# Layer 1's first products of two token tiles by seven block products in place of eight, and all element-wise work behind attention on VectorE

## The chip, the cores and the metric

The kernel runs on one core of a Trainium2 chip. The metric is the device time of one execution, in microseconds (us). Times named "profiled" are those of one execution that the hardware profiler recorded. Engines: TensorE (PE, with its weight loads as PEld), VectorE (DVE), ScalarE (ACT), GpSimd (POOL), and SyncE (SP), which here only issues transfers.

## The reference

Linear attention with decay over blocks of 64 tokens, then two feed-forward layers on the 1536 tokens x 512 channels that it gives. The two layers are where most of the work lies:

```python
x = attn_out.transpose(0, 2, 1, 3).reshape(1536, 512)
h = x @ w_in                                    # 512 x 2048, layer 0
g = np.where(h > 0.0, h, np.exp(np.minimum(h, 0.0)) - 1.0)
x = g @ w_out                                   # 2048 x 512
h = x @ w_in2                                   # layer 1
g = np.maximum(h, 0.0) + np.log1p(np.exp(-np.abs(h)))
out = g @ w_out2
```

## The kernel before

**Tiles and chunks.** Tokens lie in three tiles of 512 (t = 0, 1, 2), the 2048 inner channels of a layer in 16 chunks of 128 (c). For each layer, tile and chunk there is a first product (`hps`, 128 x 512, over 512 input channels in four parts), an activation, and a second product that is added to the tile's four accumulators `y`. A value of 32 bits is split into a high and a low part (`xh`, `xl`; `wih`, `wil`; `woh`, `wol`; `g`), and each product is three matmuls (`product`, lines 387 to 389; `m2_part`, line 437). A first product is thus 12 matmuls, a second product too.

**Stages.** Attention runs first, with the first eight chunks of tile 0 between its steps (`early_step`). Behind it `build` makes a list of operations `Op` for all the rest, and `schedule` puts them in order: it plays the operations with a table of assumed durations, keeps a list of ready ones for each engine, and writes each engine's instructions in the order in which they began. TensorE chooses between two sequences, first products (`m1_seq`) and second ones (`m2_seq`). On the chip each engine then runs its own list in order and waits where an operand or a buffer isn't ready. `PLAN` is the order of the chunks: four chunks of tile 0 (`one`), then two pairs of chunks for tiles 1 and 2 (`two` or `fast`).

**A fast pair.** `quick` computes the first products of two chunks for tiles 1 and 2, which are a 2 x 2 block product (halves of the input channels by the two chunks), with seven products of half the depth, six matmuls each, instead of four of 12. It works on sums of weight halves (`sum_ops`, tiles `sumsw`, split into `s0h`, `s0l`, `s1h`, `s1l`) and on sums of token halves (`t1` to `t4`, high and low parts). Products go to the banks `pa`, `pb` and `pd`; copies and adds of VectorE and ScalarE (`copy_op`, `add_op`, tiles `p1`, `u2`, `p5`) combine them. In each pair the sixth product (`t3`) ends on `pa`, an add on VectorE reads `pa`, and only then may the seventh (`t4`) go on in that bank. In the kernel before, layer 0 has seven fast pairs, layer 1 none. Layer 0's token sums are made from the halves of x behind attention (`first_sums`).

**Activation.** Layer 0: two steps on ScalarE, one on VectorE (line 450). Layer 1: |h| (`e`, line 741), exp, + 1 (`u`) and log (line 754) on ScalarE; then u − 1 − e (line 758), v − u (line 545), max(h, 0) + v (line 764). Then ScalarE copies the high part of `g` and the low part is v − g (line 545). Nine buffers `v` hold values in work, three hold `g`.

**VectorE or GpSimd.** The operations through `minus` and `plus` (lines 545 and 548), such as the low parts, v − u and the sums, could go to either engine in the kernel before: the one that was free first in the scheduler's play took it.

**The end.** The last accumulators are evicted (line 1099) and stored by SyncE; a `probe` of 15 matmuls stands behind the last second product.

Of the kernel before, what the change touches and what calls it, by code (L numbers as in the profile page):

```python
# [9 lines left out]
F32 = mybir.dt.float32  # L10
# [22 lines left out]

FAST = (True, False)

# [20 lines left out]
def body(ctx, tc, lamc, attqk, attkv, w1, w2, out):  # L56
# [398 lines left out]
    order = count()  # L455

    class Op:

        def __init__(self, on, key, fn, after=(), gate=None, end=None):
            self.on, self.key, self.fn, self.gate, self.done = on, key, fn, gate, end  # L460
            self.then, self.wait, self.n, self.gone, self.first = [], 0, next(order), False, False
            self.behind(*after)
            ops.append(self)
# [7 lines left out]
    def schedule(pe, free):  # L471
# [3 lines left out]
        heads = [0] * len(pe)  # L475
        pool = [0.0]

# [6 lines left out]
        def begin(op, e):  # L484
            op.gone = True
            took = op.on[e]
            if e == "V" and isinstance(took, tuple):
                took, both = took
                if both and pool[0] > now:
                    over = pool[0] - now  # L490
                    took = over + took - SHARE * over if SHARE * over < took else took / SHARE
            if e == "G":
                pool[0] = now + took
            op.fn(e) if len(op.on) > 1 else op.fn()
            busy, late = took if isinstance(took, tuple) else (took, took)
# [8 lines left out]
        while left:  # L504
            now, _, op = heappop(events)
            if op is not None:
                left -= 1
                if op.done:
                    op.done()
                for nxt in op.then:  # L510
                    nxt.wait -= 1
                    if nxt.wait == 0:
                        enter(nxt)
            if events and events[0][0] <= now:
                continue
            if free["P"] <= now:
                m2_seq, m1_seq = pe
                ahead = list(takewhile(lambda o: o.wait == 0, m2_seq[heads[0]:heads[0] + 8]))
                can = [bool(ahead), heads[1] < len(m1_seq) and m1_seq[heads[1]].wait == 0]
                can[1] = can[1] and (m1_seq[heads[1]].gate is None or m1_seq[heads[1]].gate())  # L520
                if can[0] and (not can[1] or sum(o.on["P"] > MM3 for o in ahead) + sum(o.on["P"] == MM3 for o in ahead) // 4 >= PILE and not m1_seq[heads[1]].first):
                    pick = 0
                else:
                    pick = 1 if can[1] else None
                if pick is not None:
                    heads[pick] += 1
                    begin(pe[pick][heads[pick] - 1], "P")
            for e in "SAGV":
                if free[e] > now:
                    continue  # L530
                ready[e] = [x for x in ready[e] if not x[2].gone]
                for x in ready[e]:
# [17 lines left out]
    engines = {"V": V, "G": G}  # L550
    both = {"G": TT_G, "V": TT_V}
    half = {"G": 0.76, "V": (0.42, True)}
    wide = {"G": 2.7, "V": (1.28, True)}

    def build():
# [54 lines left out]
        def weights_ops():  # L610
            for k, task in enumerate(tasks):
# [45 lines left out]
                o2 = Op({"A": SCALAR}, key, a2, [o1, summed_[t1] if t1 else None])  # L657
                o3 = Op({"V": 0.55}, key, v1, [o1])
                o4 = Op({"V": 0.75}, key, v2, [o3, o2])
                o5 = Op({"A": SCALAR}, key, a3, [o4])  # L660
                o6 = Op(W_LO, key, v3, [o5])
                loads[task] = ld, o2
# [51 lines left out]
        def act_ops(key, src, after, done):  # L714

# [3 lines left out]
            if layer == 0:  # L719
# [12 lines left out]
                o = Op({"A": SCALAR}, k, x2, [o])  # L732
                o = Op({"V": PS_V}, k, x3, [o], end=done)
            else:
# [33 lines left out]
                o = Op({"A": SCALAR}, k, s2, [o])  # L768
                o = Op(PLUS_ONE, k, s3, [o])
                o4 = Op({"A": SCALAR}, k, s4, [o])  # L770
                o5 = Op({"V": PS_V}, k, s5, [o4])
                o6 = Op(SOFT, k, s6, [o5], end=lambda: eu.append(box["i"]))
                o = Op({"V": PS_V}, k, s7, [o6], end=done)

# [9 lines left out]
            h = Op({"A": SCALAR}, k, hi, [o, m2_last.get(queue[j - 3])])  # L784
            low = Op(V_LO, k, lo, [h], end=lambda: vfree.add(box["k"]))
            for p in m2_ops[key]:
# [43 lines left out]
        def sum_ops(q):  # L830
# [26 lines left out]

            o0 = Op(W_SUM, k0, g0, deps)
            o1 = Op(W_HALF, k0, g1, deps)
            o2 = Op(W_HALF, k0, g2, deps)  # L860
            o3 = Op(W_HALF, k0, lambda e: plus(e, cut(0), cut(3), cut(0)), [o1, o2])
            o4 = Op(W_HALF, k1, lambda e: minus(e, cut(3), cut(1), cut(3)), [o0, o3])
            o5 = Op(W_HALF, k0, lambda e: minus(e, cut(1), cut(0), cut(1)), [o4])
            o6 = Op(W_HALF, k1, lambda e: minus(e, cut(2), cut(2), cut(1)), [o5])
            out_ = []
            for i, key, deps in ((0, k0, [o5, o3]), (1, k1, [o6, o4])):
# [16 lines left out]
        def quick(layer, p):  # L883
# [47 lines left out]
            def copy_op(src, tag, key, after):  # L931
# [33 lines left out]
            held["s", 0], held["s", 1] = [p5, p6], [p3, p7]  # L965
            held["p1"] = [act_ops(keys[0, 1], lambda: box["p1"], [a11], None)]
            held["u2"] = [act_ops(keys[0, 2], lambda: box["u2"], [a12], None)]
            held["p5"] = [act_ops(keys[1, 2], lambda: box["p5"], [a22], None)]
            act_ops(keys[1, 1], lambda: box["a"], [p4], lambda: give_bank(box["a"]))
# [12 lines left out]
        def part_ops(i, k, f, key, deps, new):  # L982
# [10 lines left out]
            h = Op({"A": SCALAR}, key, hi, deps)  # L993
            return h, Op(T_LO, key, lo, [h])

        def first_sums(plain_end):
# [10 lines left out]
            def chain(name, key, deps, *terms):  # L1007
                o = None
                for i, (fn, a, b) in enumerate(terms):
# [67 lines left out]
        def unit_ops(u):  # L1077
# [8 lines left out]
            for m in range(KD):  # L1086
# [15 lines left out]
                if fresh:  # L1102
# [21 lines left out]
        def split_ops(t):  # L1124
# [4 lines left out]
            for m in range(KD):  # L1129
# [10 lines left out]
                prev = h if m == 0 else prev  # L1140
                xdone[1, t].append(Op(V_LO, key0 + m * MM3 - 3.0, lo, [h]))
            held["acc", t] = list(xdone[1, t])


# [12 lines left out]
        def close_units(keys_done):  # L1157
            while made_units[0] < len(units) and all(k in keys_done or queue.index(k) < EARLY for k in units[made_units[0]]):
# [4 lines left out]
                if t in ysplit and (1, t) not in xdone:  # L1163
                    split_ops(t)

# [45 lines left out]
    def close_attention():  # L1211
# [3 lines left out]
        late["tp"] = ctx.enter_context(tc.tile_pool(name="ltp", bufs=1, reuse_waits="tile"))  # L1215

    def probe():
        ps = pp.tile([P, TT], F32, tag="b0", name="probe")
        a, x = halves["i", 2 * NF - 1][0][:, 0:P], xh[0][0]
        b = x.rearrange("p a n -> p (a n)")  # L1220
        for n in (256, 384, 512):
            for i in range(5):
                T.matmul(ps[:, :n], a, b[:, :n], start=True, stop=True, skip_group_check=True)

# [125 lines left out]
```

## Time and profile before

| | us |
|---|---|
| median of three runs | 591.49 (590.26 to 592.46) |
| the profiled execution's own time | 590.46 |
| its span from the first to the last instruction | 588.7 |
| TensorE busy | 573.4 |
| VectorE busy | 414.9 |
| ScalarE busy | 368.4 |
| GpSimd busy | 316.7 |

The span is 1.8 us shorter than the execution's own time, and that time 1.0 us shorter than the median. A matmul's record overlaps the next one's, so that a busy TensorE shows only where it did not wait.

### The profile page before, as it was taken

To read this page: it belongs to the slowest core of one execution; us is meant where nothing else is said; L and a number is where in the kernel's file an instruction comes from. 1 tells how busy PE (TensorE), PEld (TensorE's weight loads), DVE (VectorE), ACT (ScalarE), POOL (GpSimd) and SP (SyncE) were. 2 spreads that over 40 slices of the span, in tenths; PEclk is the share of its full clock that TensorE was granted. 3 is DMA by queue.
4 is the path that set the end of the run, shared out by engine and by line. 5 is a ranking of instruction groups with operands and counts; after the bars stand their busy time and mean duration, and the time that the engine had idled before them with its cause. 6 is when DMAs were issued, how large, how long until landed. Compare 5 with 4: busy or idle time off the path is not lost.

```text
span 588.7 us, 8054 instructions
## 1 busy us (share of the span) xinstructions
PE 573.4 (97%) x2999; PEld 467.9 (79%) x2999; DVE 414.9 (70%) x546; ACT 368.4 (63%) x652; POOL 316.7 (54%) x246
## 2 busy tenths in 40 slices
PE   8899999979999989999999999999999999999999
PEld 7777778757788878888888788887888887888887
DVE  6678778999868398845887937687785479633732
ACT  1365657647876667645868568887794488464720
POOL 4634356998755374544374835547453555343541
PEclk9999999989999999999999999999999999999999
DMA  8944642101214122420223102132223011000023
GB/s 317 409 165 126 243 157 90 37 0 36 73 45 135 38 70 72 144 72 1 84 96 107 37 1 72 36 108 71 73 71 108 1 37 36 1 0 1 0 85 130
DMA packets 14582, 49.80 MB, mean 85 GB/s; under 512 B 1744, under 2 KB 1744, under 8 KB 14544
## 3 DMA queue, kind: packets, MB, share of 16 engines
q1 hardware_dynamic: 14544, 49.30, 24.3%
q8 instruction: 23, 0.38, 0.3%
q14 instruction: 15, 0.12, 0.1%
HBM read 46.14 MB, written 3.15 MB: 84 GB/s over the span
## 4 chain that ended last, share of the span: by engine, by line
PE 63%; DVE 20%; ACT 5%; DMA 5%; POOL 3%; issue 3%; SPq 0%; DVEq 0%; ACTq 0%
PE y L437 31%; PE hps L387 8%; PE hps L388 8%; PE hps L389 8%; DMA raw<-w 4%; DVE r L164 2%; PE pa L387 2%; PE pa L389 2%; PE pa L388 2%; DVE sums L545 2%; DVE u L758 2%; DVE v L450 2%; DVE r L642 2%; DVE r L637 2%; DVE yacc L1099 1%
## 5 line engine op out<-in xcount | busy, mean ns | idle before, releaser
L545 POOL TENSOR_TENSOR g<-v,g 128x512 fp32r<-128x512 f32 x69 | 96.1, 1393 | 98.2 <-ACT g L777 98.2
L437 PE MATMUL y<-g,woh 128*128 128x512 f32 x384 | 119.4, 392 | 0.8 <-ACT yacc L1094 0.8
L437 PE MATMUL y<-woh,g 128*128 128x512 f32 x384 | 118.2, 389 | 0.0
L777 ACT ACTIVATE g<-v 128x512 fp32r<-128x512 f32 x89 | 56.1, 631 | 73.7 <-PE y L437 68.6
L545 POOL TENSOR_TENSOR v<-v,u 128x512 f32<-128x512 f32 x38 | 52.9, 1392 | 61.7 <-DVE u L758 61.7
L437 PEld LDWEIGHTS y<-g,woh 128*128 128x128 f32 x384 | 71.6, 188 | 17.1 <-ACT yacc L1094 1.6
L437 PEld LDWEIGHTS y<-woh,g 128*128 128x128 f32 x384 | 72.1, 188 | 14.9
L387 PE MATMUL hps<-xh,wih 128*128 128x512 f32 x200 | 79.6, 398 | 0.8 <-DVE v L764 0.6
L388 PE MATMUL hps<-xl,wih 128*128 128x512 f32 x200 | 78.3, 391 | 0.4 <-POOL xl L545 0.4
L389 PE MATMUL hps<-xh,wil 128*128 128x512 f32 x200 | 78.1, 391 | 0.0
L437 PE MATMUL y<-g,wol 128*128 128x512 f32 x192 | 74.8, 389 | 0.0
L437 PE MATMUL y<-wol,g 128*128 128x512 f32 x192 | 74.7, 389 | 0.0
L1099 DVE TENSOR_TENSOR yacc<-y,yacc 128x512 f32<-128x512 f32 x68 | 45.4, 687 | 35.9 <-PE y L437 35.8
L758 DVE SCALAR_TENSOR_TENSOR u<-u,e 128x512 f32<-128x512 f32 x48 | 43.6, 908 | 32.4 <-ACT v L754 32.4
L642 DVE CUSTOM_DVE_ANT_0 r<-r,c 128x1024 uint16<-128x1024 uint16 x49 | 46.8, 956 | 6.7 <-ACT c L632 6.1
L387 PEld LDWEIGHTS hps<-xh,wih 128*128 128x128 f32 x200 | 37.8, 189 | 11.8 <-DVE v L764 2.7
L764 DVE SCALAR_TENSOR_TENSOR v<-hps,v 128x512 f32<-128x512 f32 x48 | 32.8, 684 | 18.2 <-POOL v L545 18.0
L388 PEld LDWEIGHTS hps<-xl,wih 128*128 128x128 f32 x200 | 37.8, 189 | 8.2 <-POOL xl L545 0.8
L389 PEld LDWEIGHTS hps<-xh,wil 128*128 128x128 f32 x200 | 37.7, 188 | 7.9
L437 PEld LDWEIGHTS y<-wol,g 128*128 128x128 f32 x192 | 36.0, 188 | 7.5
L437 PEld LDWEIGHTS y<-g,wol 128*128 128x128 f32 x192 | 36.0, 188 | 7.5
L741 ACT ACTIVATE e<-hps 128x512 f32<-128x512 f32 x48 | 28.2, 587 | 16.0 <-PE hps L389 15.0
(198 smaller groups left out, 1158.4 us busy)
## 6 DMA issues: line engine op xcount, KB each, us to landing
raw<-w SPq DMA_DIRECT2D x64, 512.0 KB, 3.7
qk<-attqk SPq DMA_DIRECT2D x8, 512.0 KB, 7.0
kv<-attkv SPq DMA_DIRECT2D x8, 512.0 KB, 7.0
out<-yacc SPq DMA_DIRECT2D x12, 256.0 KB, 2.1
early<-attkv SPq DMA_DIRECT2D x2, 512.0 KB, 9.2
early<-attqk SPq DMA_DIRECT2D x2, 512.0 KB, 10.6
earlykv<-attkv SPq DMA_DIRECT2D x2, 512.0 KB, 10.9
earlyqk<-attqk SPq DMA_DIRECT2D x2, 512.0 KB, 10.9
```

What stands on the lines that cost most here:

```text
L164: V.tensor_tensor(out=ri, in0=ri, in1=c, op=ALU.add)
L387: T.matmul(ps, wh[:, wo[i]], xa[i], start=(start and i == 0), stop=False, skip_group_check=True)
L388: T.matmul(ps, wh[:, wo[i]], xb[i], start=False, stop=False, skip_group_check=True)
L389: T.matmul(ps, wl[:, wo[i]], xa[i], start=False, stop=(stop and i == n - 1), skip_group_check=True)
L437: T.matmul(yps[m], a, b, start=(begins(key) and i == 0), stop=(ends(key) and i == 2))
L545: engines[e].tensor_tensor(out=o, in0=a, in1=b, op=ALU.subtract)
L642: V.tensor_tensor(out=ri, in0=ri, in1=box["c"], op=ALU.add)
L741: A.activation(out=box["e"], in_=src(), func=AF.Abs)
L758: V.scalar_tensor_tensor(out=u, in0=u, scalar=-1.0, in1=box["e"], op0=ALU.add, op1=ALU.subtract)
L764: V.scalar_tensor_tensor(out=box["v"], in0=src(), scalar=0.0, in1=box["v"], op0=ALU.max, op1=ALU.add)
L777: A.activation(out=g[:, 0], in_=box["v"], func=AF.Copy)
L1099: V.tensor_tensor(out=y, in0=yps[m], in1=y, op=ALU.add)
```

## The change

- `FAST = (True, True)`: layer 1's eight pairs of chunks for tiles 1 and 2 are fast pairs too.
- `second_sums` makes layer 1's token sums out of the accumulators of layer 0 (`yacc`): it keeps the split parts of x that plain products still need, and writes differences of the accumulators over them, where `split_ops` only split them before. Layer 0's `first_sums` computes what it did.
- The tables that name the engines of an operation (`W_LO`, `V_LO`, `SOFT` and so on) hold VectorE alone. GpSimd keeps its work inside attention and gets none behind it.
- The scheduler's assumed durations change, and with them its model of what VectorE and GpSimd do to each other.
- The probe is gone.

```diff
-FAST = (True, False)
+FAST = (True, True)
...
-    MM3, SCALAR, TT_V, TT_G, PS_V = 0.68, 0.65, (0.71, True), 1.4, (0.71, False)
-    SHARE, PILE = 0.35, 2
+    MM3, SCALAR, SB_V, SB_G, PS_V = 0.68, 0.635, (0.69, True), (1.295, True), (0.69, False)
+    PIPE = {"P": 0.0, "A": 0.1, "V": 0.08, "G": 0.04, "S": 0.0}
+    PILE, QUEUE = 2, 3
...
+        def second_sums():
...
+            def sub(key, out_, a, b, deps):
+                return Either(V_LO, key, lambda e: minus(e, out_(), a(), b()), deps)
...
+                f3 = Either(V_LO, pos[2], t3, [y[2, i], y[2, 2 + i]] + held.get(("p1", "p5")[i], []))
+                f1 = sub(pos[2], yy(2, i), yy(2, i), yy(1, i), [f3, y[1, i]])
+                f2 = sub(pos[3], yy(2, 2 + i), yy(2, 2 + i), yy(2, i), [f1, k22])
+                f4 = sub(pos[6], yy(1, 2 + i), yy(1, 2 + i), yy(2, 2 + i), [f2, k21])
+                for n, f, o in ((1, yy(2, i), f1), (2, yy(2, 2 + i), f2), (3, lambda i=i: tmp[i], f3), (4, yy(1, 2 + i), f4)):
+                    h, low = part_ops(n, i, f, pos[{1: 2, 2: 3, 3: 5, 4: 6}[n]], [o, prior.get(n)] + clear, i == 0)
...
                 if t in ysplit and (1, t) not in xdone:
-                    split_ops(t)
+                    if t == 0 or not FAST[1]:
+                        split_ops(t)
+                    elif t == 1:
+                        second_sums()
...
-    W_LO = both
-    V_LO = both
-    W_SUM, W_HALF, W_SLO = both, half, both
-    T_LO, T_SUM = both, both
-    SOFT = both
+    W_LO = {"V": SB_V}
+    V_LO = {"V": SB_V}
+    W_SUM, W_HALF, W_SLO = {"V": SB_V}, {"V": half["V"]}, {"V": SB_V}
+    T_LO, T_SUM = {"V": SB_V}, {"V": SB_V}
+    SOFT = {"V": SB_V}
...
-        probe()
```

The whole program has 2645 matmuls before and 2582 after, 548 and 860 instructions on VectorE, 251 and 46 on GpSimd, 654 and 703 on ScalarE.

What stands in the engines' lists, at three places. First VectorE of the changed kernel, behind attention, where the first fast pair of layer 0 ends: `p1`, `u2` and `p5` are the adds that combine its products, `sumsw` the next pair's weight sums, `r` a weight in conversion.

```order
L949 TENSOR_TENSOR p1_1371<-pb_1288,p1_1371 128x512
L553 TENSOR_TENSOR sumsw_1397<-wih4_738,wil4_740 128x512
L553 TENSOR_TENSOR sumsw_1397<-wih5_851,wil5_853 128x256 x2
L641 TENSOR_SCALAR r_1165<-r_1165 128x512
L553 TENSOR_TENSOR sumsw_1397<-sumsw_1397 128x256
L450 SCALAR_TENSOR_TENSOR v0_1399<-v0_1399,p1_1371 128x512
L949 TENSOR_TENSOR u2_1408<-pd_1377,u2_1408 128x512
L550 TENSOR_TENSOR sumsw_1397<-sumsw_1397 128x256
L949 TENSOR_TENSOR p5_1394<-pa_1276,p5_1394 128x512
```

The last row, the add that reads `pa`, is the 61st instruction behind attention's last; in the kernel before, part of what stands in front of it was GpSimd's.

Second, VectorE in the middle of layer 1. Before, two keys' steps (line 758 and line 764) and a unit's evictions (line 1099):

```order
L758 SCALAR_TENSOR_TENSOR u0_4298<-u0_4298,e0_4292 128x512
L764 SCALAR_TENSOR_TENSOR v8_4293<-hps_4171,v8_4293 128x512
L1099 TENSOR_TENSOR yacc2_3700<-y1_4239,yacc2_3700 128x512
L1099 TENSOR_TENSOR yacc2_3701<-y2_4245,yacc2_3701 128x512
L758 SCALAR_TENSOR_TENSOR u1_4328<-u1_4328,e1_4322 128x512
L764 SCALAR_TENSOR_TENSOR v1_4323<-hps_4197,v1_4323 128x512
L1099 TENSOR_TENSOR yacc2_3702<-y3_4251,yacc2_3702 128x512
```

And in the changed kernel, where the same steps are lines 762, 550 and 768:

```order
L762 SCALAR_TENSOR_TENSOR u1_3492<-u1_3492,e1_3469 128x512
L949 TENSOR_TENSOR p5_3479<-pa_3369,p5_3479 128x512
L550 TENSOR_TENSOR v1_3470<-v1_3470,u1_3492 128x512
L550 TENSOR_TENSOR wil5_3531<-r_3450,wih5_3507 128x512
L768 SCALAR_TENSOR_TENSOR v1_3470<-p1_3433,v1_3470 128x512
L762 SCALAR_TENSOR_TENSOR u0_3528<-u0_3528,e0_3510 128x512
L550 TENSOR_TENSOR g2_3544<-v0_3336,g2_3544 128x512
L550 TENSOR_TENSOR v2_3511<-v2_3511,u0_3528 128x512
L550 TENSOR_TENSOR wol5_3566<-r_3339,woh5_3497 128x512
L768 SCALAR_TENSOR_TENSOR v2_3511<-u2_3460,v2_3511 128x512
```

What stood on GpSimd beside the first list, v − u, the low parts of `g` and of the weights, stands in VectorE's own list now, with the adds of the fast pair, and one key's three steps stand with another instruction between them.

Third, TensorE in layer 1's first fast pair of the changed kernel: the end of the sixth product, second products `y` of another key, and the start of the seventh.

```order
L389 MATMUL pa_3271<-t3h_3175,s1l_2838 128x512
L437 MATMUL y0_3205<-woh3_2887,g0_3242 128x512 x2
L437 MATMUL y0_3205<-wol3_2962,g0_3242 128x512
L437 MATMUL y1_3212<-woh3_2887,g0_3242 128x512 x2
L437 MATMUL y1_3212<-wol3_2962,g0_3242 128x512
L387 MATMUL pa_3271<-t4h_3302,wih5_2441 128x512
```

Six matmuls of a second product stand between the two, where the first fast pair of layer 0 has none.

## Rows read from the trace of the kernel before

**Rows 1.** The page: engines (busy, share, instructions), a group (busy, mean ns), a transfer.

```profile
PE 573.4 (97%) x2999; PEld 467.9 (79%) x2999; DVE 414.9 (70%) x546; ACT 368.4 (63%) x652; POOL 316.7 (54%) x246
...
L777 ACT ACTIVATE g<-v 128x512 fp32r<-128x512 f32 x89 | 56.1, 631 | 73.7 <-PE y L437 68.6
...
out<-yacc SPq DMA_DIRECT2D x12, 256.0 KB, 2.1
```

**Rows 2.** The chain that ended last: start us, us, what.

```profile
554.29 30.60 PE y L437 x135
```

**Rows 3.** Busy time by stretch: width, each engine (instructions), granted clock, transfers.

```profile
94.70:150.00 55.30, 49.20 (x204) 38.65 (x203) 53.17 (x52) 34.28 (x61) 50.45 (x37) 0.97 0.11 35
150.00:332.60 182.60, 180.94 (x797) 149.21 (x797) 136.79 (x178) 123.77 (x219) 101.73 (x81) 1.00 0.22 74
332.60:550.50 217.90, 216.61 (x950) 177.22 (x948) 141.32 (x179) 151.87 (x272) 107.90 (x77) 1.00 0.13 44
...
126.00:130.00 4.00, 4.00 (x13) 3.09 (x11) 4.00 (x5) 1.84 (x4) 4.00 (x4) 0.57 0.00 0
...
480.00:500.00 20.00, 19.36 (x86) 15.72 (x85) 18.98 (x20) 15.86 (x30) 11.45 (x8) 1.00 0.16 53
```

**Rows 4.** TensorE's timeline, 118 to 134 us: start, us, instruction [idle before <-releaser].

```profile
120.98 0.39 PE L437 MATMUL y<-g,wol 128*128 128x512 f32 x1
125.54 0.50 PE L387 MATMUL pd<-t1h,s0h 128*128 128x512 f32 x1 [4.18 <-DVE v L450]
...
126.47 0.63 PE L387 MATMUL pd<-t1h,s0h 128*128 128x512 f32 x1
...
133.76 0.50 PE L387 MATMUL pa<-t4h,wih 128*128 128x512 f32 x1 [0.85 <-DVE p L945]
```

**Rows 5.** Groups of VectorE and GpSimd, 94.7 to 150 us: busy us, mean ns.

```profile
L545 DVE TENSOR_TENSOR sumsw<-sumsw 128x256 f32<-128x256 f32 x3 | 4.5, 1511 | 0.0
...
L545 DVE TENSOR_TENSOR sums<-xh2b,xh2a 128x512 f32<-128x512 f32 x2 | 3.5, 1774 | 0.0
...
L548 POOL TENSOR_TENSOR sumsw<-wih,wil 128x512 f32<-128x512 f32 x3 | 5.1, 1701 | 0.1
```

**Rows 6.** VectorE's timeline, 409 to 430 us.

```profile
411.44 0.42 DVE L637 TENSOR_SCALAR r<-r 128x512 uint32<-128x512 uint32 x1
411.77 0.69 DVE L758 SCALAR_TENSOR_TENSOR u<-u,e 128x512 f32<-128x512 f32 x1
412.38 0.69 DVE L545 TENSOR_TENSOR wol<-r,woh 128x512 fp32r<-128x512 f32 x1
...
420.03 0.68 DVE L758 SCALAR_TENSOR_TENSOR u<-u,e 128x512 f32<-128x512 f32 x1
420.63 0.69 DVE L764 SCALAR_TENSOR_TENSOR v<-hps,v 128x512 f32<-128x512 f32 x1
...
424.82 0.69 DVE L758 SCALAR_TENSOR_TENSOR u<-u,e 128x512 f32<-128x512 f32 x1
425.55 0.69 DVE L545 TENSOR_TENSOR v<-v,u 128x512 f32<-128x512 f32 x1
```

**Rows 7.** The timeline of the program's end.

```profile
582.88 2.73 DVE L1099 TENSOR_TENSOR yacc<-y,yacc 128x512 f32<-128x512 f32 x4 [8.15 <-PE y L437]
...
583.60 2.37 SPq L1114 DMA_DIRECT2D out<-yacc  x4
...
584.72 2.79 PE L1223 MATMUL probe<-xh,wih 128*128 128x256 f32 x15
```

**Rows 8.** Groups of VectorE and GpSimd, 332.6 to 550.5 us: busy, mean ns, idle before, releaser.

```profile
L758 DVE SCALAR_TENSOR_TENSOR u<-u,e 128x512 f32<-128x512 f32 x41 | 37.5, 915 | 29.7 <-ACT v L754 29.7
L764 DVE SCALAR_TENSOR_TENSOR v<-hps,v 128x512 f32<-128x512 f32 x40 | 27.4, 685 | 18.2 <-POOL v L545 18.0
...
L545 POOL TENSOR_TENSOR v<-v,u 128x512 f32<-128x512 f32 x33 | 46.4, 1406 | 52.5 <-DVE u L758 52.5
```

More of the change, by code (lines that the diff above doesn't have):

```diff
@@ L475, in schedule @@
         heads = [0] * len(pe)
-        pool = [0.0]
+        port = {"V": 0.0, "G": 0.0}
         def enter(op):
@@ L486, in begin @@
             took = op.on[e]
[L487 to L495, printed above, removed]
+            op.fn(e) if op.names else op.fn()
+            if e in "VG":
+                took, shared = took
+                if shared:
+                    took += max(0.0, port["VG"[e == "V"]] - now - 0.14)
+                    port[e] = now + took
+            busy, late = took if isinstance(took, tuple) else (took - PIPE[e], took)
             free[e] = now + busy
@@ L520, in schedule @@
                 can[1] = can[1] and (m1_seq[heads[1]].gate is None or m1_seq[heads[1]].gate())
-                if can[0] and (not can[1] or sum(o.on["P"] > MM3 for o in ahead) + sum(o.on["P"] == MM3 for o in ahead) // 4 >= PILE and not m1_seq[heads[1]].first):
+                if can[0] and (not can[1] or sum(o.on["P"][0] for o in ahead) / (4 * MM3) >= PILE and not m1_seq[heads[1]].first):
                     pick = 0
@@ L531, in schedule @@
                 ready[e] = [x for x in ready[e] if not x[2].gone]
+                if e == "G" and sum(not x[2].gone for x in ready["V"]) < QUEUE:
+                    continue
                 for x in ready[e]:
@@ L550, in body @@
     engines = {"V": V, "G": G}
-    both = {"G": TT_G, "V": TT_V}
-    half = {"G": 0.76, "V": (0.42, True)}
-    wide = {"G": 2.7, "V": (1.28, True)}
+    both = {"V": SB_V, "G": SB_G}
+    half = {"V": (0.415, True), "G": (0.74, True)}
     def build():
@@ L784, in act_ops @@
             h = Op({"A": SCALAR}, k, hi, [o, m2_last.get(queue[j - 3])])
-            low = Op(V_LO, k, lo, [h], end=lambda: vfree.add(box["k"]))
+            low = Either(V_LO, k, lo, [h], end=lambda: vfree.add(box["k"]))
             for p in m2_ops[key]:
@@ L993, in part_ops @@
             h = Op({"A": SCALAR}, key, hi, deps)
-            return h, Op(T_LO, key, lo, [h])
+            return h, Either(T_LO, key, lo, [h])
         def first_sums(plain_end):
@@ L1140, in split_ops, with keep, hi, lo @@
                 prev = h if m == 0 else prev
-                xdone[1, t].append(Op(V_LO, key0 + m * MM3 - 3.0, lo, [h]))
+                xdone[1, t].append(Either(V_LO, key0 + m * MM3 - 3.0, lo, [h]))
             held["acc", t] = list(xdone[1, t])
+        def second_sums():
+            p = next(p for kind, layer, p in PLAN if kind == "fast" and layer == 1)
+            pos = [nom[1, p, "P", k] - 3.0 for k in range(7)]
+            y = {(t, m): o for t in (1, 2) for m, o in enumerate(ysplit[t])}
+            clear = xuse[1] + xuse[2]
+            done = {i: [] for i in (1, 2, 3, 4)}
+            xdone[1, 1], xdone[1, 2] = [None] * KD, [None] * KD
+            made_x = {}
+            reads = {1: [], 2: []}
+            tmp = {}
+            prior = {}
+            def keep(t, m, key):
+                def hi():
+                    if t not in made_x:
+                        made_x[t] = True
+                        new_x(t, 1)
+                    A.activation(out=xh[t][m // 2][:, m % 2], in_=yacc[0, t][m], func=AF.Copy)
+                def lo(e):
+                    minus(e, xl[t][m // 2][:, m % 2], yacc[0, t][m], f32(xh[t][m // 2][:, m % 2]))
+                h = Op({"A": SCALAR}, key, hi, [y[t, m]] + clear)
+                o = Either(V_LO, key, lo, [h])
+                xdone[1, t][m] = o
+                reads[t].append(o)
+                return o
+            def sub(key, out_, a, b, deps):
+                return Either(V_LO, key, lambda e: minus(e, out_(), a(), b()), deps)
+            def yy(t, m):
+                return lambda: yacc[0, t][m]
+            for i in range(2):
+                def tmp_new(i=i):
+                    tmp[i] = late["hp"].tile([P, TT], F32, tag=("p1", "p5")[i], name="sums3")
+                k11 = keep(1, i, pos[0])
+                k21 = keep(1, 2 + i, pos[1])
+                k22 = keep(2, 2 + i, pos[3])
+                def t3(e, i=i, tmp_new=tmp_new):
+                    tmp_new()
+                    minus(e, tmp[i], yacc[0, 2][2 + i], yacc[0, 2][i])
+                f3 = Either(V_LO, pos[2], t3, [y[2, i], y[2, 2 + i]] + held.get(("p1", "p5")[i], []))
[4 more added lines that the diff above has]
+                    h, low = part_ops(n, i, f, pos[{1: 2, 2: 3, 3: 5, 4: 6}[n]], [o, prior.get(n)] + clear, i == 0)
+                    prior[n] = h
+                    done[n].append(low)
+                    if n == 3:
+                        held[("p1", "p5")[i]] = [low]
+                reads[2] += [f1, f2, done[1][-1], done[2][-1], f3]
+                reads[1] += [f1, f4, done[4][-1]]
+                reads[2] += [f4]
+            held["acc", 1], held["acc", 2] = reads[1], reads[2]
+            tdone[1] = done
@@ L1215, in close_attention @@
         late["tp"] = ctx.enter_context(tc.tile_pool(name="ltp", bufs=1, reuse_waits="tile"))
[L1217 to L1223, printed above, removed]
     def start():
```

55 lines of the change are left out of this document (29 added, 26 removed).

## The prediction

> **What bounds the kernel now.** I read the page first. TensorE is busy 97% of the span, VectorE 70% [rows 1]. With TensorE that full, only two things can move the time: the number of matmuls, and the waits left between them. The pitch of a matmul is in the chain that ended last: 135 in 30.60 us, 0.2267 us each [rows 2].
>
> Then the stretches [rows 3]. Their bounds are places of the program: 94.7 is where attention's last VectorE instruction ends, 332.6 and 550.5 are evictions that close the same accumulations in both kernels. At 0.2267 us per matmul TensorE loses 55.3 − 204 × 0.2267 = 9.1 us in 94.7 to 150, 1.9 us up to 332.6, and 2.5 us up to 550.5: 13.5 us in all. The timeline of TensorE says where the 9.1 went [rows 4]: the product `pd` on the first token sums waited 4.18 us for VectorE, then matmuls took 0.63 us instead of 0.39 at a granted clock of 0.57 between 126 and 130 us, the mark of a stretch partly at 1.2 instead of 2.4 GHz [rows 3, 4], and `t4` waited 0.85 us more. In those 55.3 us VectorE is busy 53.17 and GpSimd 50.45 [rows 3]: both are full there, and TensorE waits for them. Later VectorE is idle a third of the time (141.32 of 217.9).
>
> VectorE and GpSimd stretch each other. On two SBUF tensors VectorE takes 1.77 us for 128x512 and 1.51 for 128x256, and GpSimd 1.70 for 128x512, while both are full [rows 5]. Where GpSimd is still, the same VectorE instruction takes 0.69 us for 128x512 and 0.42 for a tensor_scalar, and the next one begins before it ends: from start to start 0.61 (411.77 to 412.38), 0.60 (420.03 to 420.63), and 0.33 behind the tensor_scalar [rows 6]. For 128x256 no free row stands there; I take 0.33 too, since the tensor_scalar has the same short form; the other bound is half of 1.51.
>
> **The change, part by part.** *Fewer matmuls.* A pair of chunks of layer 1 takes 4 products of 12 matmuls before, 7 of 6 now. Over 8 pairs that is 48 fewer: 48 × 0.2267 = **−10.9 us**, if TensorE stays as full.
>
> *The probe.* Its 15 matmuls end at 584.72 + 2.79 = 587.5. Beside them run the last evictions (to 585.6) and the last four stores, issued until 583.60 + 2.37 = 586.0 and landing 2.1 us later, at 588.1 [rows 1, 7]. The stores end later than the probe: removing it is worth **0**; without that cover it would be worth at most 587.5 − 586.0 = 1.5 us less the landing, so nothing either.
>
> *GpSimd's work on VectorE.* 205 instructions leave GpSimd; with the block scheme's own, VectorE goes from 548 to 860. At the first place nothing is added, the 61 instructions that the order shows from attention's end to the add that reads `pa` and releases `t4` are about what both engines issued up to then. 49 are wide, 12 short: 49 × 0.60 + 12 × 0.335 = 33.4 us, so VectorE gets there at 94.7 + 33.4 + 0.1 = 128.2. It was idle 2.1 of 55.3 us in this stretch [rows 3]; that share adds 1.3: 129.5. TensorE could begin `pd` at 121.2 (120.98 + 0.23) and `t4` 24 matmuls later, at 126.6. So it waits 2.9 us, and `t4` begins at 129.5 instead of 133.76 [rows 4]: −4.2 us. What is late next is no longer `pd` (its last operand `s0l` is 32 instructions in, near 112) but the add on `pa`. A single wait of 2.9 us lies between waits of 0.85 that left the clock alone and the 4.18 behind which it fell [rows 4]; half the slow matmuls' cost (14 × 0.2 = 2.8) is my allowance: +1.4. From there to 332.6 the order has 224 wide and 71 short VectorE instructions, 158 us, beside 858 matmuls, 194.5 us: VectorE has room, and I halve the 1.9 us lost there: −1.0. Layer 0 together: **−3.8 us**.
>
> *Layer 1.* Here the cover is thin. Between the evictions that close layer 0 and the one that stood at 550.5, the new order has 840 matmuls, 190.4 us, and 277 wide and 56 short VectorE instructions: 277 × 0.60 + 56 × 0.335 = 185.0 us. VectorE must be busy 97% of the time or TensorE waits. About a dozen instructions follow directly on one whose result they read; from start to start such a pair takes 0.73 instead of 0.60 (424.82 to 425.55) [rows 6], 1.5 us more. In its fullest stretches VectorE was idle 3.9% (94.7 to 150) and 5.1% (480 to 500) [rows 3]. At 4% the 186.5 us become 194.3: TensorE waits 3.9 us, where it lost 2.5. **+1.4 us.** Bounds: 0 wait if the nine `v` buffers cover VectorE's delays; 15 us at 10% idle. I stay near 4% because the fullest rows do. ScalarE gets 49 more instructions in the whole program, at most 0.63 us each or 31 us [rows 1]; with all of them in layer 1 its 151.87 us [rows 3] would be 183 of 190, so it stays under VectorE's load. Behind the last boundary TensorE has 216 matmuls for 52 VectorE instructions: no wait.
>
> One rule of the Trainium skill speaks against this count. Its page "VectorE: DVE Perf Modes", section "The DRAIN you can't avoid", says that the next operation does not start until the pipe is empty; it adds that some start earlier. The trace disagrees with the strict form: 0.60 to 0.61 from start to start for a duration of 0.69 [rows 6]. By the strict rule layer 1 would be 277 × 0.69 + 56 × 0.42 = 215 us of VectorE, and the forecast the last rival's.
>
> **Sum:** 590.46 − 10.9 − 3.8 + 1.4 = **577.2 us**, against the profiled execution's own time. That execution is 1.0 us under the median of the runs; a median at the same place would read 578.
>
> **Rivals.** *VectorE is covered in layer 1 as well.* For it: nine `v` buffers and three-deep `g` let TensorE run on while VectorE is late, and at every point that I summed there VectorE is ahead of the matmul that needs it. Then neither the 3.9 nor the 1.4 comes: about 572; with all 13.5 us of waits gone, 590.46 − 10.9 − 13.5 = 566.
>
> *VectorE is the bound in layer 1.* Every GpSimd instruction removed there lay off the path (GpSimd waited 52.5 us for VectorE's `u` [rows 8]), and all of them now stand in one queue with the evictions. At 10% idle 186.5 becomes 207.2, 16.8 us over TensorE instead of 3.9: 590.1, no change. Against it: VectorE's idle time here was waiting for GpSimd (18.0 us in front of the `max` at L764 [rows 8]), which ends, and its 0.92 us per `u` [rows 8] falls to 0.69.
>
> *Slower.* One mechanism: VectorE's instructions do not overlap in the new queue, because neighbours wait for each other (`u`, `v − u`, `max` of one key all on one engine). Then the pitch is the duration, 0.69 and 0.42: 214.7 us against 190.4 costs 24.3 instead of 3.9, and the first stretch 38.9 instead of 33.4: 577.2 + 20.4 + 5.5 = 603. It decides from a pitch of about 0.67 on, where layer 1 has lost what the rest gains. Against it: the order puts another key's instruction between most such pairs.
>
> **How the numbers follow.** Forecast 0.60 (572 to 583); covered 0.15 (565 to 572); bound 0.20 (583 to 593); slower 0.05. The forecast is the likeliest case's time, 577. The range 568 to 588 leaves out a part of the covered case, the upper half of the bound case, and the slower one, about 0.2 together. A change under about 0.5%, 3 us, cannot be told from none here. Faster than 588.5: 0.60 + 0.15 + half of the bound case and a little more, 0.87; within 3 us: 0.08; slower: 0.05.
>
> **What would show it.** In the new profile: 48 and 15 fewer matmuls; VectorE's wide instructions at 0.69 or less everywhere behind 95 us and GpSimd empty; `t4` of the first fast pair beginning near 129 with VectorE's add as its releaser; VectorE busy over 93% between the two evictions of layer 1, TensorE waiting there 2 to 6 us in many pieces, most for VectorE. It is wrong if `pd` still waits, if VectorE's mean for 128x512 on SBUF stays near 0.9, or if TensorE loses over 10 us in layer 1.

## The result and the profile after

| | before | after |
|---|---|---|
| median, us | 591.30 (590.26 to 592.46, 4 runs) | 574.26 (573.62 to 574.62, 4 runs) |
| ratio to before, 95% interval | | 0.971 (0.969 to 0.973) |
| the profiled execution's own time, us | 590.46 | 574.03 |

The forecast was 577.0 us, range 568 to 588. The execution's own time fell by 16.43 us; the forecast's sum had 13.3.

The page of the kernel after: engines (busy, share, instructions), then two groups of layer 1's activation (busy us, mean ns, idle before).

```profile
PE 558.0 (97%) x2936; PEld 458.3 (80%) x2936; DVE 489.4 (86%) x858; ACT 390.9 (68%) x701; POOL 41.2 (7%) x41
...
L762 DVE SCALAR_TENSOR_TENSOR u<-u,e 128x512 f32<-128x512 f32 x48 | 32.7, 684 | 4.2 <-ACT v L758 4.1
...
L550 DVE TENSOR_TENSOR v<-v,u 128x512 f32<-128x512 f32 x48 | 32.8, 684 | 0.2
```

63 matmuls are gone, as the sum has it. The step `u` fell from 915 to 684 ns, and v − u, GpSimd's at 1406 ns before, takes 684 on VectorE [rows 8].

The same stretches as [rows 3], bounded by the same places of the program: attention's end is at 95.3 now, the eviction that closes layer 0 at 326.8, the one that stood at 550.5 at 519.7. Columns as there.

```profile
326.80:519.70 192.90, 191.21 (x841) 157.48 (x840) 188.61 (x333) 159.60 (x292) 0.00 (x0) 1.00 0.16 50
519.70:572.30 52.60, 48.26 (x213) 39.62 (x212) 32.76 (x52) 22.90 (x39) 0.00 (x0) 0.99 0.16 61
150.00:326.80 176.80, 176.80 (x782) 146.34 (x781) 146.69 (x262) 124.75 (x223) 0.00 (x0) 1.00 0.24 78
95.30:150.00 54.70, 51.43 (x219) 41.72 (x218) 52.04 (x96) 35.98 (x64) 0.00 (x0) 0.97 0.09 30
...
124.50:128.00 3.50, 3.50 (x10) 2.73 (x9) 2.81 (x7) 1.94 (x4) 0.00 (x0) 0.51 0.00 0
```

The reader is to see three things. Layer 0, with 1001 matmuls in both kernels, takes 231.5 us from attention's end in place of 237.9: 6.4 less, of which a later end of attention gives back 0.6. In layer 1 VectorE is busy 188.61 of 192.9 us, and still TensorE loses only 192.9 − 841 × 0.2267 = 2.2 us, as much as before (2.5). And between 150 and 326.8 us TensorE waits for nothing.

TensorE's timeline at the place of [rows 4]: start, us, instruction, idle before and its releaser.

```profile
120.15 0.39 PE L437 MATMUL y<-g,wol 128*128 128x512 f32 x1
123.02 0.50 PE L387 MATMUL pd<-t1h,s0h 128*128 128x512 f32 x1 [2.48 <-DVE v L450]
...
124.91 0.63 PE L388 MATMUL pa<-t2l,s0h 128*128 128x512 f32 x1
...
131.17 0.50 PE L387 MATMUL pa<-t4h,wih 128*128 128x512 f32 x1 [0.78 <-DVE p L949]
```

`pd` still waits, 2.48 us where it waited 4.18. Behind the wait six matmuls go at full speed, then nine are slow, seven of them at 0.63 us: the granted clock is 0.51 there (last line of the windows above), mostly 1.2 instead of 2.4 GHz. What `pd` waits for stands in VectorE's timeline of the same stretch:

```profile
112.51 0.68 DVE L550 TENSOR_TENSOR s0l<-sumsw,s0h 128x512 fp32r<-128x512 f32 x1
...
115.06 0.68 DVE L553 TENSOR_TENSOR sums<-sums,xl2b 128x512 f32<-128x512 f32 x1
115.67 0.68 DVE L550 TENSOR_TENSOR sums<-xh2b,xh2a 128x512 f32<-128x512 f32 x1
...
122.29 1.28 DVE L450 SCALAR_TENSOR_TENSOR v<-v,hps 128x512 f32<-128x512 f32 x2
...
130.43 0.69 DVE L949 TENSOR_TENSOR p<-pa,p 128x512 f32<-128x512 f32 x1 [0.34 <-PE pa L389]
```

The operands are there in time: `s0l`, the last, ends at 113.2. The releaser is L450, the last step of a plain chunk's activation, which is the last reader of a bank of products (the first of the two in its row; `pd` begins as it ends). `pd` doesn't read the `v` that L450 writes: it waits for that **bank**. [rows 4] names the same releaser for the 4.18 us before. From 115 to 122 us VectorE makes token sums that only later products read, each 0.60 from the one before, and L450 stands behind them.

### The profile page after: what moved, and what is told of

Same layout as the page of the kernel before. It is cut to its first block, busy times and chain, and to the rows that moved or that the text cites. A ratio compares the mean times of both kernels' runs of the same rounds, so it can differ in the third digit from the quotient of the medians.

```text
span 572.3 us, 7939 instructions
## 1 busy us (share of the span) xinstructions
PE 558.0 (97%) x2936; PEld 458.3 (80%) x2936; DVE 489.4 (86%) x858; ACT 390.9 (68%) x701; POOL 41.2 (7%) x41
## 4 chain that ended last, share of the span: by engine, by line
PE 91%; DVE 6%; DMA 1%; ACT 1%; issue 0%; SPq 0%; ACTq 0%
PE y L437 43%; PE hps L387 6%; PE hps L389 6%; PE hps L388 6%; PE pa L387 4%; PE pa L389 4%; PE pa L388 4%; PE pd L387 2%; PE pd L388 2%; PE pd L389 2%; PE xps L327 2%; PE sps L302 2%; PE xps L322 2%; PE pb L389 1%; PE pb L387 1%; PE pb L388 1%
## 5 line engine op out<-in xcount | busy, mean ns | idle before, releaser
L550 DVE TENSOR_TENSOR g<-v,g 128x512 fp32r<-128x512 f32 x89 | 60.8, 685 | 19.0 <-ACT g L781 18.8
L387 PE MATMUL hps<-xh,wih 128*128 128x512 f32 x136 | 54.4, 400 | 0.0
L388 PE MATMUL hps<-xl,wih 128*128 128x512 f32 x136 | 53.3, 392 | 0.0
L389 PE MATMUL hps<-xh,wil 128*128 128x512 f32 x136 | 53.2, 391 | 0.0
L646 DVE CUSTOM_DVE_ANT_0 r<-r,c 128x1024 uint16<-128x1024 uint16 x49 | 33.5, 685 | 1.7 <-ACT c L636 1.2
L632 ACT ACTIVATE r<-raw 128x512 f32<-128x512 f32 x49 | 32.6, 665 | 3.3 <-DVE wol L550 2.2
L550 DVE TENSOR_TENSOR v<-v,u 128x512 f32<-128x512 f32 x48 | 32.8, 684 | 0.2
L636 ACT ACTIVATE c<-raw 128x512 uint32<-128x512 uint32 x49 | 32.5, 663 | 0.3 <-DVE r L646 0.2
L758 ACT ACTIVATE v<-u 128x512 f32<-128x512 f32 x48 | 30.0, 627 | 0.4
L447 ACT ACTIVATE e<-e 128x512 f32<-128x512 f32 x48 | 30.1, 627 | 0.3
## 6 DMA issues: line engine op xcount, KB each, us to landing
earlykv<-attkv SPq DMA_DIRECT2D x2, 512.0 KB, 10.9
earlyqk<-attqk SPq DMA_DIRECT2D x2, 512.0 KB, 10.9
```

The source lines that it names most:

```text
L387: T.matmul(ps, wh[:, wo[i]], xa[i], start=(start and i == 0), stop=False, skip_group_check=True)
L388: T.matmul(ps, wh[:, wo[i]], xb[i], start=False, stop=False, skip_group_check=True)
L389: T.matmul(ps, wl[:, wo[i]], xa[i], start=False, stop=(stop and i == n - 1), skip_group_check=True)
L447: A.activation(out=o, in_=a, func=AF.Exp, scale=-1.0)
L550: engines[e].tensor_tensor(out=o, in0=a, in1=b, op=ALU.subtract)
L632: A.activation(out=r, in_=high.bitcast(F32), func=AF.Prelu, scale=2.0 ** -112, alpha=-2.0 ** 32)
```

## The experiments

Times are medians; the kernel before, run beside them, had medians of 591.45 to 592.24 us, and ratios are to it.

**GpSimd idle alone.** `idle_only`:

```diff
-FAST = (True, True)
+FAST = (True, False)
```

> Half of the change: VectorE alone behind attention, but layer 1 with plain products (48 matmuls more than the full change). Theory A (GpSimd's work stretched VectorE, and both were late in the first stretch behind attention): TensorE has 10.9 us more than in the full change and waits as little there, at most 1 us in layer 1, so 583 to 585.5 us, 6 to 8 under the kernel before. Rival (GpSimd's instructions lay off the path, and all of the gain is the matmuls): 589 to 592, no change.

581.94 us, ratio 0.982 (0.979 to 0.985): about 10 us from VectorE alone, more than its share of the forecast. The windows of that kernel, layer 1 and layer 0:

```profile
326.80:540.00 213.20, 213.20 (x942) 176.50 (x941) 155.93 (x251) 152.19 (x273) 0.00 (x0) 1.00 0.13 45
...
95.30:150.00 54.70, 51.43 (x219) 41.72 (x218) 51.96 (x96) 35.62 (x65) 0.00 (x0) 0.97 0.09 30
```

The first stretch is that of the kernel after, and in layer 1, where VectorE has 155.93 us for 213.2, TensorE waits for nothing; before's 2.5 us of waits there [rows 3] went with GpSimd's share of the work.

**The block scheme alone**, on the kernel before, with its sharing, its durations and its probe. `scheme_only`:

```diff
-FAST = (True, False)
+FAST = (True, True)
...
+        def second_sums():
...
-                    split_ops(t)
+                    if t == 0 or not FAST[1]:
+                        split_ops(t)
+                    elif t == 1:
+                        second_sums()
```

> The other half: layer 1 by the block scheme, but with VectorE and GpSimd sharing the work and the scheduler's old durations, the probe still there. Theory A: the 333 instructions between the two evictions of layer 1 go at the rate of the stretch 94.7 to 150 of the kernel before, where 89 took 55.3 us, 0.62 us each: 207 us against 190 us of matmuls, so TensorE waits some 10 to 17 us more there and gains 10.9: 588 to 597 us. Rival (the block scheme pays by its 48 matmuls whoever does the element-wise work): 579 to 582.

608.52 us, ratio 1.028 (1.025 to 1.031): slower, by more than I expected. 48 fewer matmuls, and the kernel loses 17 us. The window of layer 1 (columns as above, GpSimd the fifth engine), then groups of VectorE and GpSimd between 330 and 560 us:

```profile
350.00:560.00 210.00, 191.10 (x809) 153.05 (x808) 185.68 (x216) 154.88 (x281) 147.68 (x110) 0.98 0.13 43
```

```profile
L758 DVE SCALAR_TENSOR_TENSOR u<-u,e 128x512 f32<-128x512 f32 x39 | 41.2, 1060 | 9.4 <-ACT v L754 9.4
...
L764 DVE SCALAR_TENSOR_TENSOR v<-p,v 128x512 f32<-128x512 f32 x13 | 15.0, 1153 | 1.6 <-POOL v L545 1.6
L764 DVE SCALAR_TENSOR_TENSOR v<-hps,v 128x512 f32<-128x512 f32 x14 | 9.4, 680 | 1.6 <-POOL v L545 1.6
...
L545 POOL TENSOR_TENSOR v<-v,u 128x512 f32<-128x512 f32 x30 | 43.5, 1450 | 33.3 <-DVE u L758 32.6 <-ACT r L628 0.7
```

VectorE is busy 185.68 of 210 us for 216 instructions; alone it does 333 in 188.61. `u` takes 1060 ns in place of 684. The two lines of L764 show where the stretching lies: the same step takes 1153 ns on `p`, which lies in SBUF as `v` does, and 680 on `hps`, which lies in a bank of products. TensorE loses 210 − 809 × 0.2267 = 26.6 us. This run has the old durations as well as the sharing; the next one parts them.

**Sharing alone**, with the new durations. `both_new` lets the planner choose GpSimd again:

```diff
-    W_LO = {"V": SB_V}
+    W_LO = both
-    V_LO = {"V": SB_V}
+    V_LO = both
...
-    SOFT = {"V": SB_V}
+    SOFT = both
```

(`W_SUM`, `W_HALF`, `W_SLO`, `T_LO` and `T_SUM` likewise.)

> The changed kernel with the tables that let VectorE or GpSimd take the element-wise work, under the scheduler's new durations and model: 148 instructions of its list go to GpSimd, the rest is the same. Theory A (a GpSimd instruction costs VectorE more by the shared access to SBUF than it saves it): TensorE waits more, 580 to 600. Rival (the loss of the block scheme with GpSimd came from the old durations' order): 570 to 577.

589.82 us, ratio 0.997 (0.995 to 0.999): nearly the whole gain is gone, 15.6 us against the kernel after. GpSimd has 210 instructions in the profile in place of 41, 169 more and not 148. The same sharing took 608.52 us with the old durations (`scheme_only`), so these have a part in that run's loss. Who TensorE waits for (us in total, times, longest), and groups of both engines between 330 and 520 us:

```profile
PE pd L387 <- DVE v L450: 5.2, 1, 5.2
PE pa L387 <- ACT p L940: 4.8, 1, 4.8
...
PE pa L387 <- DVE p L949: 2.0, 2, 1.3
```

```profile
L762 DVE SCALAR_TENSOR_TENSOR u<-u,e 128x512 f32<-128x512 f32 x34 | 38.1, 1125 | 0.0
...
L550 POOL TENSOR_TENSOR v<-v,u 128x512 f32<-128x512 f32 x16 | 25.3, 1579 | 12.5 <-DVE u L762 12.5
```

The wait in front of `pd` doubles, and the stretched instructions are back, 1125 and 1579 ns. The Trainium skill's page "SBUF — State Buffer", section "Who interferes with whom", states that a VectorE instruction with two SBUF inputs contends with a GpSimd instruction that reads SBUF; 1125 ns here and 684 without GpSimd agree. It gives no price for a kernel; this run does.

**The assumed durations.** I had listed them in the change and given them no price. `old_durations` (VectorE alone, block scheme in both layers):

```diff
-    MM3, SCALAR, SB_V, SB_G, PS_V = 0.68, 0.635, (0.69, True), (1.295, True), (0.69, False)
-    PIPE = {"P": 0.0, "A": 0.1, "V": 0.08, "G": 0.04, "S": 0.0}
+    MM3, SCALAR, SB_V, SB_G, PS_V = 0.68, 0.65, (0.71, True), (1.4, True), (0.71, False)
+    PIPE = {"P": 0.0, "A": 0.0, "V": 0.0, "G": 0.0, "S": 0.0}
```

> The changed kernel with the scheduler's old durations (0.65 for ScalarE, 0.71 for VectorE, nothing for the overlap of neighbours), VectorE alone behind attention. Theory A (the durations only shift the order a little): 573 to 577. Rival (a good part of the gain is the new durations' order): 579 or more.

595.96 us, ratio 1.009 (1.006 to 1.012). My theory fell: with the old durations the changed kernel is slower than before, 21.7 us slower than with the new ones, with the same instructions, of which nine copies have gone from ScalarE to VectorE. The next three runs ask which number, and why.

`pipe_zero` changes the second line alone (PIPE is what the planner takes off an instruction's duration to get the time for which it holds its engine):

```diff
-    PIPE = {"P": 0.0, "A": 0.1, "V": 0.08, "G": 0.04, "S": 0.0}
+    PIPE = {"P": 0.0, "A": 0.0, "V": 0.0, "G": 0.0, "S": 0.0}
```

> The changed kernel with PIPE at zero alone: in the scheduler's play an instruction occupies VectorE for its whole 0.69 us and ScalarE for 0.635, where the trace has 0.60 and 0.52 from start to start. Theory (the play believes VectorE overloaded in layer 1: 277 x 0.69 + 56 x 0.415 = 214 us against 190 of TensorE, so TensorE's list is written for a late VectorE): 588 to 598, nearly all that the old durations cost, with TensorE's waits in layer 1 and at the end. Rival (the longer latencies of 0.65 and 0.71 did it): 573 to 578.

589.97 us, ratio 0.996 (0.994 to 0.998). `pipe_kept` changes the first line alone:

```diff
-    MM3, SCALAR, SB_V, SB_G, PS_V = 0.68, 0.635, (0.69, True), (1.295, True), (0.69, False)
+    MM3, SCALAR, SB_V, SB_G, PS_V = 0.68, 0.65, (0.71, True), (1.4, True), (0.71, False)
```

> The changed kernel with the old 0.65, 0.71 and 1.4, but the new PIPE. Theory: the play then has 277 x 0.63 + 56 x 0.335 = 193 us of VectorE against 190, hardly overloaded: 574 to 582. Rival (the longer latencies did it): 588 to 598.

573.28 us, ratio 0.967 (0.964 to 0.970), as fast as the kernel after. `idle_old` has both old lines, and plain products in layer 1:

```diff
-FAST = (True, True)
+FAST = (True, False)
...
-    PIPE = {"P": 0.0, "A": 0.1, "V": 0.08, "G": 0.04, "S": 0.0}
+    PIPE = {"P": 0.0, "A": 0.0, "V": 0.0, "G": 0.0, "S": 0.0}
```

> No fast pairs in layer 1, VectorE alone, all old durations with PIPE at zero. Theory (the durations matter only where the play's VectorE is overloaded, and without layer 1's sums it has room: about 250 instructions there, 175 us, beside 942 matmuls, 214 us): within 3 us of the same kernel with the new durations, 579 to 585. Rival (another order is worse wherever it differs): over 588, no gain left against the kernel before.

581.94 us, ratio 0.982 (0.979 to 0.986), the median of `idle_only` to the hundredth; so the 10 us of that run don't come from the durations. PIPE is what costs, and only with the fast pairs of layer 1, where the engines are nearly full: all three runs came out as the theory of the overload had it. One thing they don't part: `pipe_zero` takes PIPE from ScalarE too. At 0.635 us ScalarE's 292 instructions of layer 1 make 185 us, just under TensorE's 190, and VectorE's 214 are over it. That speaks for VectorE, but no run has its PIPE alone at zero. Where the time goes, `pipe_zero`:

```profile
330.00:520.00 190.00, 183.06 (x793) 147.73 (x792) 173.13 (x301) 147.12 (x265) 0.00 (x0) 1.00 0.15 51
520.00:588.80 68.80, 60.27 (x255) 48.35 (x253) 52.44 (x89) 37.81 (x65) 0.00 (x0) 0.96 0.14 51
```

and `pipe_kept` over the same stretches:

```profile
330.00:520.00 190.00, 188.26 (x829) 155.03 (x828) 185.92 (x327) 156.65 (x283) 0.00 (x0) 1.00 0.15 50
520.00:571.30 51.30, 46.91 (x207) 38.50 (x206) 34.97 (x56) 24.03 (x41) 0.00 (x0) 0.99 0.17 62
```

With PIPE at zero TensorE loses 190 − 793 × 0.2267 = 10.2 us in the body of layer 1 (2.1 in `pipe_kept`), and VectorE isn't the one that is full: it is busy 173.13 us where it could be 185.92. By the count in the expectation, the play's VectorE had 214 us of work for 190 of TensorE, so the lists were written for a VectorE that is always late; what was put off, 89 instructions in place of 56, falls behind 520 us, where TensorE loses 11.0 us (4.4 in `pipe_kept`, the last stores in both). On the chip the engines then wait for each other; what TensorE waits for behind 330 us, and VectorE between 330 and 520 (us in total, times, longest):

```profile
PE y L437 <- ACT g L781: 3.8, 2, 2.8
PE pa L387 <- DVE p L949: 2.4, 3, 0.8
PE y L437 <- DVE g L550: 2.3, 5, 0.6
```

```profile
DVE g L550 <- ACT g L781: 4.1, 11, 0.9
DVE yacc L1100 <- PE y L437: 3.3, 3, 2.2
DVE u L949 <- PE pd L389: 3.3, 4, 1.4
```

**The wait for the bank.** `bank_early`, on the kernel after, makes a plain chunk's three steps in layer 0 due 5 us behind the place of its first product, where that is earlier than the place of its second product, which set it so far:

```diff
+                ka = min(k, nom.get(key, 1e9) + EARLIER)
-                o = Op({"A": SCALAR}, k, x1, after, v_gate(key))
+                o = Op({"A": SCALAR}, ka, x1, after, v_gate(key))
...
-                o = Op({"V": PS_V if bank else SB_V}, k, x3, [o], end=done)
+                o = Op({"V": PS_V if bank else SB_V}, ka, x3, [o], end=done)
...
+    EARLIER = 5.0
```

> The changed kernel, with one edit to the scheduler's priorities: the steps that empty the bank of a plain first product get a due time 5 us behind that product, and no longer that of the second product that uses it. Theory A (the wait of pd for the bank of a product whose VectorE step stood behind the token sums cost 2.5 us, and the slow clock behind it 1.9): pd starts without a wait, the clock holds, and 3 to 5 us go: 569.5 to 571.5. Rival (VectorE's list is full there, so that the wait only moves to t4 and to the later sums): 573 to 575.

569.50 us, ratio 0.962 (0.960 to 0.964): 4.8 us faster than the kernel after, and the fastest version here. TensorE's timeline, then VectorE's step that frees the bank:

```profile
113.36 0.39 PE L387 MATMUL pd<-t1h,s0h 128*128 128x512 f32 x1
...
126.54 0.50 PE L387 MATMUL pa<-t4h,wih 128*128 128x512 f32 x1 [0.78 <-DVE p L950]
```

```profile
111.11 0.68 DVE L450 SCALAR_TENSOR_TENSOR v<-v,hps 128x512 f32<-128x512 f32 x1
```

`pd` begins without a wait, no matmul behind it is slow, and `t4` begins 4.6 us earlier. That is the 2.65 us of the wait and 1.8 of slow matmuls that the kernel after still had. The play also moved TensorE's own order: 30 matmuls of second products that stood in front of `pd` now stand behind its first six. They take the same time on either side.

`bank_before` is the same edit on the kernel before.

> The kernel before with the edit of priorities alone: the steps that empty the bank of a plain first product are due 5 us behind it. Theory A (there too pd waited for a bank whose VectorE step stood far back, and the clock fell behind that wait): 3 to 7 us less, 584.5 to 588.5. Rival (with GpSimd at work both engines are full there, and the wait moves to the next operand): 590 to 593.

591.20 us, ratio 1.000 (0.998 to 1.001): nothing. TensorE's timeline, then ScalarE's:

```profile
115.34 0.39 PE L387 MATMUL pd<-t1h,s0h 128*128 128x512 f32 x1
...
127.91 0.79 PE L387 MATMUL pa<-t2h,s0h 128*128 128x512 f32 x1 [4.71 <-ACT p L937]
...
135.46 0.50 PE L387 MATMUL pa<-t4h,wih 128*128 128x512 f32 x1 [1.63 <-DVE p L946]
```

```profile
123.91 0.63 ACT L989 ACTIVATE t3h<-sums 128x512 fp32r<-128x512 f32 x1 [6.14 <-POOL sums L545]
...
127.26 0.60 ACT L937 ACTIVATE p<-pa 128x512 f32<-128x512 f32 x1 [1.13 <-POOL t3l L545]
```

The wait of 4.18 us is gone from the start of `pd` (0.61 is left within it, for `s0l`) and stands, as 4.71, in front of the next product: ScalarE, which must copy `pa` first, is held by GpSimd's token sums. With VectorE and GpSimd both full there, the new order only moved the wait.

`copies_early`, on `bank_early`, makes a fast pair's three copies due 2 us sooner:

```diff
-            k1 = copy_op("a", "p1", pos[3] - 1.0, [p1])
+            k1 = copy_op("a", "p1", pos[3] - 3.0, [p1])
...
-            k2 = copy_op("a", "u2", pos[5] - 1.0, [p6])
+            k2 = copy_op("a", "u2", pos[5] - 3.0, [p6])
```

> The changed kernel with the plain product's steps of layer 0 due by their bank (as in the run before that moved them) and, new, the three copies of a fast pair due 3 us before their place in TensorE's list in place of 1 us. If the one wait of 0.9 us for a copy of pd near 351 us is a matter of its due time: 568.5 to 569, at the edge of what can be told from the run that moved the steps alone (569.5). Rival (VectorE is full there, so what moves ahead delays something else): 569.5 to 573.

569.97 us (569.05 to 572.21), ratio 0.963 (0.958 to 0.967): no difference from `bank_early` that can be told.

**How much cover layer 1 has.** `plus_one_v` moves ScalarE's + 1, a 128x512 tensor_scalar of each key, to VectorE, 48 instructions more:

```diff
-    PLUS_ONE = {"A": SCALAR}
+    PLUS_ONE = {"V": half["V"]}
```

> The changed kernel with layer 1's + 1 step on VectorE instead of ScalarE: 48 short instructions more on VectorE, 36 of them between the two evictions of layer 1, 36 x 0.335 = 12 us on 185 us, beside 190.4 us of matmuls. Theory A (VectorE is only just covered there): its 197 us are over TensorE's, which waits 7 to 14 us more: 581 to 588. Rival (VectorE has cover enough, and the wait of layer 1 has another cause): 574 to 576.

576.01 us (574.40 to 578.35), ratio 0.975 (0.972 to 0.977): 1.8 us above the kernel after. I had expected 581 and more. Its windows, the whole of layer 1's body and a later one:

```profile
326.00:518.00 192.00, 191.04 (x842) 157.50 (x841) 190.52 (x352) 140.00 (x248) 0.00 (x0) 1.00 0.15 50
...
549.00:560.00 11.00, 9.08 (x29) 6.23 (x28) 9.20 (x16) 3.69 (x7) 0.00 (x0) 0.84 0.14 53
```

VectorE is busy 190.52 of 192 us, and TensorE loses 1.1. What VectorE could not do there slipped behind the border (74 instructions after 518 us, where the kernel after has 52 behind the same place), and TensorE's waits came at 549 to 560 us. From the end of layer 0 (326.0 us) to the end of its profiled execution this run takes 576.43 − 326.0 = 250.4 us, where the kernel after takes 247.2, 3.2 less. The medians differ by 1.8 alone; in this profiled execution the slow matmuls of layer 0 stayed away (last section).

**The probe.** `probe_back` puts its 15 matmuls behind the last second product again:

```diff
         build()
+        probe()
```

> The changed kernel with the 15 matmuls behind the end put back. Theory A (the last stores land later than they end): 574.3 us, within 0.8. Rival (the program's end waits for them): 1.5 to 2.6 us more, 576 to 577.

575.08 us (572.14 to 575.46), ratio 0.969 (0.967 to 0.972): the same as the kernel after, as the prediction had it.

## Why the prediction came out

**Matmuls, −10.9: right.** Layer 1 from its first boundary to the end of the execution took 590.46 − 332.6 = 257.9 us and takes 574.03 − 326.8 = 247.2: 10.6 less.

**Layer 0, −3.8: 5.8 measured** (332.6 to 326.8). Up to `t4` the size was right and the mechanism wrong. With its allowance the sum had `t4` at 129.5 + 1.4 = 130.9, and it began at 131.17; but the step "What is late next is no longer `pd`" failed, and with it one of the prediction's own signs of being wrong came true. I had checked the operands of `pd` (`s0l` ends at 113.2, where I had it near 112), not its bank, whose last reader L450 the planner had put late, though [rows 4] names L450. Instead of one wait of 2.9 us for the add on `pa` there were 2.65 at `pd`, 1.8 of slow matmuls and 0.94 at `t4`, each counted from start to start beyond 0.2267. `bank_early` shows it: with the bank in time `t4` begins at 126.54. The count of VectorE's list was right: VectorE came to the add at 130.09 (its row above: 130.43 less 0.34 of waiting for the product), which is my 129.5 and the 0.6 of attention's later end. But TensorE, held at `pd`, had the product ready no sooner. That the waits I had missed were about as long as the one I had is luck. The allowance was miscounted too: behind the 4.18 us before, nine matmuls were slow and not 14, and lost 1.6 us and not 2.8 (126.12 to 129.77 us, 3.65 − 9 × 0.2267); in the kernel after nine lost 1.6 again, the whole and not half. The mis-sized term is "I halve the 1.9 us lost there: −1.0": from `t4` to the layer's end the gain is 5.8 − (133.76 − 131.17) = 3.2. TensorE waits for nothing there any more, neither behind 150 us nor in the piece from 133.76 to 150 that I had left out.

**Layer 1, +1.4: too dear; 0 measured.** VectorE was idle 2.2%, not 4%, and TensorE lost 2.2 us where it lost 2.5. The forecast had 3.9, the rival "covered in layer 1 as well" 0: the run lies between the two. (That rival's 572 takes layer 1's 1.4 off twice, since the 3.9 holds it; without that it is 577.2 − 3.9 = 573.3.) `plus_one_v` shows how far the cover goes: to 99% busy in this stretch, with 3.2 us more from its start to the end of the execution. The pitch carried the count: 0.60 for 128x512 (115.06 to 115.67), and 277 × 0.60 + 56 × 0.335 = 185 us did fit into 192.9. By the strict form of the rule in the Trainium skill's "VectorE: DVE Perf Modes", "The DRAIN you can't avoid", they would not have. `pipe_zero` is a planner that believes the strict form, for ScalarE too, and it costs 15.7 us.

**The split of the gain.** I gave the matmuls 10.9 and VectorE alone the small rest. Measured, VectorE alone brings about 10 us, and the block scheme on top of it 581.94 − 574.26 = 7.7. With the work shared, the scheme loses 17 us under the old durations and gains 1.6 under the new ones (`both_new`). The term for layer 0 and the 2.5 us of layer 1, which I had carried on as lost, make up 8.3 of the first (7.9 between the profiled executions, 590.46 − 582.61; the rest lies within the spread of the runs); the second is the 10.9 less the 2.2 us of waits that come back with the scheme, and 1.0 that lies within the spread of the runs. The rival "bound" (590.1) was near: `both_new` and `pipe_zero` end there, by the sharing and by the planner's numbers.

**The durations: not priced.** I read the new lists and so took their effect into the count without naming it. That the lists were written with PIPE is worth 15.7 us of the 17, as by `both_new` GpSimd's idleness is worth 15.6: without either one about 2 us of the gain are left.

What stays open: why the old 0.65 and 0.71, worth nothing while PIPE stands, cost 6 us more when PIPE is zero (595.96 against 589.97), and how much of PIPE's worth is ScalarE's.

## What to carry to other kernels

Where VectorE and GpSimd work on two SBUF operands at once, price both as stretched and compare with VectorE alone at its free pitch: here one engine at 0.60 us did more than two (333 instructions in layer 1 in 192.9 us, against 326 in 210 in `scheme_only`). Whether a sharing that gives GpSimd only a few instructions would pay was not run. A planner must hold an engine for the pitch from start to start and hand the result on after the duration; with one number for both, it saw an overload here that wasn't there and wrote a bad order for the engines that were nearly full. And a product waits for its bank as well as for its operands: the last reader of the bank needs a due time of its own.

## What the runs showed of the hardware

Two waits of TensorE of the same length, at the same place of the program, ended differently. In the kernel after, behind 2.48 us, the clock was 0.51 between 124.5 and 128 us (shown above); in `idle_only`, behind 2.48 us too, 0.66 between 123 and 128. In `plus_one_v` the same product waited as long, and the clock stayed at 1.00:

```profile
123.38 0.50 PE L387 MATMUL pd<-t1h,s0h 128*128 128x512 f32 x1 [2.48 <-DVE v L450]
```

```profile
122.00:126.00 4.00, 2.62 (x11) 2.17 (x12) 4.00 (x8) 2.10 (x4) 0.00 (x0) 1.00 0.00 0
```

In `idle_old` a wait of 3.20 us there left it at 1.00 as well:

```profile
125.37 0.47 PE L387 MATMUL pd<-t1h,s0h 128*128 128x512 f32 x1 [3.20 <-DVE v L450]
```

```profile
125.40:130.00 4.60, 4.60 (x20) 3.80 (x21) 4.20 (x8) 3.33 (x6) 0.00 (x0) 1.00 0.00 0
```

So the slow matmuls, 1.8 us in the kernel after, come or stay away by something that the length of the wait alone does not decide; my allowance of half was a coin's toss, and no run here settles it.
